# Convolution taps laid out over other steps of a fused convolution and FFN, and put between VectorE's low parts and their sum

## The chip, the cores and the metric

The kernel runs on one core of one Trainium2 chip. Its time is the device time of one execution in microseconds (us). The core has TensorE (matrix products; PE in the profile, its weight loads PEld), VectorE (DVE), ScalarE (ACT), GpSimd (POOL) and SyncE (SP, which here only issues transfers). Each engine takes its instructions in the order in which the program lists them; semaphores hold an instruction until what it needs is there.

## The reference, cut to what matters

```python
def _attn_ref(x, weight):                    # x (8, 4096, 192), weight (8, 7)
    w = weight - np.max(weight, axis=-1, keepdims=True)
    w = np.exp(w)
    w = w / (np.sum(w, axis=-1, keepdims=True) + 1e-09)
    x_pad = np.concatenate([np.zeros((B, pad, D)), x], axis=1)
    idx = np.arange(S)[:, None] + np.arange(K)[None, :]
    x_unf = x_pad[:, idx, :].reshape(B, S, K, H, group)
    out = np.einsum('hk,bskhg->bshg', w, x_unf)

def _moe_ref(x, w_in, w_out):                # (32768, 192), (192, 2048), (2048, 192)
    h = x @ w_in
    g = np.where(h >= 1, h, np.where(h <= -1, 0.0, (h + 1) ** 2 / 4))
    return g @ w_out
```

A causal convolution of seven taps along the sequence, with one set of softmax weights per head, and behind it a two-layer network on every token. All arrays are float32.

## The kernel before, in words

The 32768 tokens are cut into 64 blocks of 512 (`TB`). The 2048 hidden features of a block are taken in eight pairs of 128. One pair of one block is a step `q` of the main loop (512 steps); `j = q % 8` is its place in the block, `c, i = divmod(q, 16)` its place in a pair of blocks. I call the 16 steps of a pair of blocks a period. The convolution for a pair of blocks is done in three units: "a" (the first block's channels 0 to 127), "b" (the second block's) and "r" (the other 64 channels of both).

Float32 precision comes from splitting each operand into a high and a low part of a faster type (`float32r`). The first 16 steps (`NF32`) run the second product in plain float32 while the split weights are made; all later steps have the same shape:

- TensorE, `mm1(q)` (L405): 18 matmuls of 64 rows and 512 columns into a PSUM buffer `h`, of which there are two, so the product of step `q` needs the buffer of step `q-2` to be free again. Then `mm2(q-3)` (L458): 18 matmuls that add the second product of an earlier step into four banks.
- ScalarE, `act_both(q)` (L504): L507 and L508 make `g = ((h+1)/2 clipped at 0) ** 2`. After the last step of a block, `evac_banks` (L547) copies the four banks out (four L552, in steps i = 2 and 10). Then what the convolution asks of it, and `act_hi(q-1)` (L518): the high part `gh`.
- VectorE, `act_lo(q-2)` (L520): L524 takes the low part `gl = g - gh`, L528 adds its two halves to `m`. Then the transposes of the output (L573, in i = 6, 7, 14, 15), what the convolution asks, and last `act_most(q)` (L510, L806), which reads `h` once more and so frees its PSUM buffer.

What the convolution does in a step stands in a plan written by hand: `PLAN_B`, `PLAN_A`, `PLAN_R` (L748 to L751) give for each `i` the taps, "T" (the transpose that brings channels to partitions, L148) or "split". `conv_slot` (L759) carries it out, for b, a and r in this order. Taps of unit a are VectorE's (L213 for the first, L215 for the others). Taps of b and r are a product on ScalarE (L220; L227 for tap 0) and an add on GpSimd (L231). "split" makes the high part on ScalarE (L249, L263) and the low part on GpSimd (L253) or, for r, VectorE (L264), and SP issues the transfers that swap halves between partitions. B's transpose for the coming pair is at the very end of step 15 (L950), and its taps are in steps 0 to 5 of its own pair.

GpSimd's queue also issues the accumulating transfers that join the four banks (`evac_add`, L556, in j = 3 and 4), SP's queue the stores (`store`, L563, in j = 6 and 7) and the loads of x. The first pair of blocks has plans of its own (`FIRST_*`).

The order of the calls within a step of the steady part is what the change touches (L926 to L951):

```python
act_both(q); evac...; act_lo(n); evac_add...; store...
conv_slot(i, conv_b, conv_n.get("a"), conv_n.get("r"))
act_hi(q - 1); act_most(q)
```

Of the kernel before, what the change touches and what calls it, by code (L numbers as in the profile page):

```python
# [8 lines left out]
F32 = mybir.dt.float32  # L9
# [9 lines left out]
P = 128  # L19
TB = 512  # L20
SQ = 32
# [10 lines left out]
def lightconv_then_ffn(ctx: ExitStack, tc: tile.TileContext, x, weight, w_in, w_out, out):  # L32
# [33 lines left out]
    NPAIR = NF // 2  # L66
    DR = D - P
    NG = TB // SQ + 1
# [5 lines left out]
    stage = ctx.enter_context(tc.tile_pool(name="stage", bufs=2))  # L74
# [3 lines left out]
    xw = ctx.enter_context(tc.tile_pool(name="xw", bufs=2))  # L78
# [32 lines left out]
    def load_unit(c, u, engs=None):  # L111
        ta, tb = 2 * c * TB, (2 * c + 1) * TB
        if u == "rb":
            return load_raw([tb, tb, tb + TB // 2, tb + TB // 2], [P, P + SQ, P, P + SQ], engs,
                            TB // 2)
        if u == "r":
            return load_raw([ta, ta, tb, tb], [P, P + SQ, P, P + SQ], engs)
        return load_raw([ta if u == "a" else tb] * 4, [0, SQ, 2 * SQ, 3 * SQ], engs)
# [14 lines left out]
    NF32 = 2 * NPAIR  # L133
    SH = NG * SQ - TB - (K - 1)

    class Conv:
# [5 lines left out]
            self.n = TB // 2 if u == "rb" else TB  # L142

        def transpose(self):
            self.xT = xw.tile([P, NG * SQ], F32, name="xT")
            self.y = xw.tile([P, TB], F32, name="y")
            n = self.n + SQ
            nc.vector.transpose(out=self.xT[:, 0:n],  # L148
                                in_=self.raw.rearrange("p j b -> p (j b)")[:, 0:n])
# [155 lines left out]
    CC = max(n_all)  # L305
# [96 lines left out]
    NQ = NSB * NPAIR  # L402
    hs, g32, gs, ghs, gls, gts, accs = {}, {}, {}, {}, {}, {}, {}

    def mm1(q):  # L405

        s, j = divmod(q, NPAIR)

        if q == 0:
            h = hs[q] = [ps_o.tile([P, TB], F32, name=n) for n in ("accr1", "accm0")]  # L410
        else:
            h = hs[q] = ps_h.tile([P, 2, TB], F32, name="h")
            h = [h[:, e, :] for e in range(2)]

        if s == 0:
            mms = [(WI[j], us, [xop[s][u] for u in us]) for us in ("ns", "sn", "rr")]
        else:
            mms = [(W[j][:, part], u + u, [xop[s][u, x]] * 2) for u in "nsr"
                   for part, x in ((0, "hi"), (1, "hi"), (0, "lo"))]
        for n, (w, us, x) in enumerate(mms):  # L420
            for e in range(2):
                c0 = COL[us[e]][e]
                nc.tensor.matmul(h[e], w[HALVES[e], c0:c0 + P], x[e][e],  # L423
                                 start=(n == 0), stop=(n == len(mms) - 1))
# [5 lines left out]
    def mm2_first(q):  # L430


        s, j = divmod(q, NPAIR)
        g, w = g32.pop(q), WF[j + LAG]
        if j == 0:
            new_accs(s)
        for e in range(2):
            for b in range(TB // P):
                a, c0 = "mr"[b // 2], b % 2 * D
                for i, half in enumerate(HALVES):  # L440
                    nc.tensor.matmul(accs[s][a, i][:, c0:c0 + D], g[half, e, b * P:(b + 1) * P],  # L441
                                     w[half, e, :], start=(j == 0 and e == 0 and b % 2 == 0),
                                     stop=(j == NPAIR - 1 and e == 1 and b % 2 == 1))
# [39 lines left out]
    def tiles(q):  # L483
        return [slice(0, 1), slice(1, 2)] if q == NQ - 1 else [slice(0, 2)]
# [25 lines left out]
    def act_most(q):  # L510
        h, g = hs.pop(q), gs[q]
        for e in tiles(q):
            most(h[:, e, :], g[:, e, :])
# [3 lines left out]
        for e in tiles(q):  # L517
            nc.scalar.copy(gh[:, e, :], gs[q][:, e, :])  # L518

    def act_lo(q):  # L520
        gl = gls[q] = act.tile([P, 2, TB], F32R, name="gl", bufs=3)
        g, gh = gs.pop(q), ghs[q].bitcast(F32)
        for e in tiles(q):
            nc.vector.tensor_sub(gl[:, e, :], g[:, e, :], gh[:, e, :])  # L524
        gt = stage.tile([P, CC], F32R, name="m")[:, 0:TB]
        gts[q] = gt
        gl = gls[q].bitcast(F32)
        nc.vector.tensor_add(gt, gl[:, 0, :], gl[:, 1, :])  # L528
# [188 lines left out]
    def whole(j, *cols):  # L717
        for _ in chunks[j].bits(*cols):
# [20 lines left out]
    conv_b, conv_rb = Conv(0, "b", raw_b), Conv(0, "rb", raw_rb)  # L739
# [5 lines left out]

    PLAN_B = {0: (0, 1), 1: (2,), 2: (3,), 3: (4,), 4: (5, 6), 5: "split"}  # L748
    PLAN_A = {1: ("T",), 2: (0, 1), 3: (2,), 4: (3,), 8: (4,), 9: (5,), 10: (6,), 11: "split"}
    PLAN_R = {5: ("T",), 6: (0,), 7: (1,), 8: (2,), 9: (3,), 10: (4,), 11: (5,), 12: (6,),  # L750
              13: "split"}  # L751


    FIRST_B = {2: 2, 3: 3, 4: 4, 5: 5}
# [1 line left out]
    FIRST_A = {7: ("T", 0, 1, 2), 8: (3, 4), 9: (5, 6), 11: "split"}  # L756
    FIRST_R = {8: ("T",), 9: (0,), 10: (1, 2), 11: (3, 4), 12: (5, 6), 13: "split"}

    def conv_slot(i, b, a, r):  # L759
        early = b.c == 0  # L760
        plans = ((None if early else b, PLAN_B), (a, FIRST_A if early else PLAN_A),
                 (r, FIRST_R if early else PLAN_R))
        for u, plan in plans:
            what = plan.get(i, ()) if u else ()
            if what == "split":
                if u is r:
                    u.split_rest()
                else:
                    u.split()
                continue  # L770
            if "T" in what:
                u.transpose()
            ks = [k for k in what if k != "T"]
            if ks:
                (u.taps_dve if u is a and not early else u.taps)(*ks)
# [8 lines left out]
    def parts_hi(q):  # L784
        for n, rest in PARTS.get(q, ()):
            chunks[n].hi(rest)
# [17 lines left out]
    def most(h, g):  # L804

        nc.vector.scalar_tensor_tensor(out=g, in0=g, scalar=1.0, in1=h, op0=ALU.min, op1=ALU.max)  # L806
# [74 lines left out]
    conv_n, ahead = {}, {}  # L881
    for q in range(NQ + LATE):
        s, j = divmod(q, NPAIR)
        c, i = divmod(q, 2 * NPAIR)
        if q < NQ and i == 0 and c > 0:
            conv_b = conv_n["b"]
        if q < NQ and i == (0 if c > 0 else 4):
            conv_n, ahead = ahead, {}
            if c + 1 < NB:
                for u in "arb":  # L890
                    if u not in conv_n:
                        conv_n[u] = Conv(c + 1, u, load_unit(c + 1, u))
        if i == 14 and c + 2 < NB:
            ahead = {u: Conv(c + 2, u, load_unit(c + 2, u)) for u in "ar"}

        done = q - (DELAY if q < NF32 + DELAY else LATE)
        if done < 0 or q == NF32 + DELAY:
            done = None
        if q == NPAIR:
            mm2_first(done)  # L900
        if q < NQ:
            mm1(q)
        if done is not None and q != NPAIR:
            (mm2 if done >= NF32 else mm2_first)(done)

        if q < 2:
            (step_0, step_1)[q]()
        elif q < NPAIR:
            first_step(q)
        elif q < NF32:  # L910
            if q == NPAIR + 1:
                evac(0)
            if q == 2 * NPAIR - 2:
                pending.extend(late)
            let_go()
            act_clip(q)
            act_square(q)
            parts_hi(q + 1)
            parts_lo(q, (True,))
            let_go()  # L920
            act_max(q)
            parts_lo(q, (False,))
            conv_slot(i, conv_b, conv_n.get("a"), conv_n.get("r"))
            if j >= NPAIR - 2:
                store(0, "mr"[j - NPAIR + 2])
        else:  # L926
            if q < NQ:
                act_both(q)
            if done is not None and done % NPAIR == NPAIR - 1:
                (evac if done < NF32 else evac_banks if done < NQ - 1 else evac_last)(  # L930
                    done // NPAIR)
            if q == NF32:
                parts_lo(q)
            n = q - 1 if q < NF32 + 3 else q - 2
            if n in ghs and n not in gls:
                act_lo(n)
            if q < NQ:
                if s > 2 and j in (3, 4):
                    evac_add(s - 1, j - 3)
                m = 6 if s > 2 else 2  # L940
                if m <= j < m + 2:
                    store(s - 1, "mr"[j - m])
                conv_slot(i, conv_b, conv_n.get("a"), conv_n.get("r"))
            if q - 1 in gs and q - 1 not in ghs:
                act_hi(q - 1)
            if q < NQ:
                act_most(q)
            if q < NF32 + 2:
                act_hi(q)
        if q < NQ and i == 2 * NPAIR - 1 and conv_n:  # L950
            conv_n["b"].transpose()  # L951
        if q == NQ - 4:
            plain = ob.tile([P, TB // SQ, SQ], F32, name="osb").rearrange("p j b -> p (j b)")[:, 0:P]
            diagonal(plain, 0)
# [26 lines left out]
```

## Time and profile before

| | us |
|---|---|
| median of 3 runs | 2159.35 |
| lowest and highest | 2158.59 to 2160.54 |
| the profiled execution | 2159.94 |
| its span, first to last instruction | 2157.9 |
| TensorE busy | 2136.2 |
| VectorE busy | 1996.8 |
| ScalarE busy | 1976.9 |
| GpSimd busy | 824.8 |

The mean granted clock of TensorE is 0.999. Matmuls run in pairs on two halves of the array, so their durations overlap and TensorE's busy time is a union. In a row of the timeline stand the start, the duration, the engine, the line of the kernel, the operation and its operands; a bracket at the end gives the idle time before it and what ended that. Durations on VectorE and ScalarE can overlap by some 0.08 us with the next instruction, so distances from start to start are used for sums. An instruction that waits for more than a semaphore, for a port say, is shown longer.

### The profile page before, as it was taken

The page shows a single profiled execution, that of the slowest core. Times are in us where ns is not written, and L with a number is a line of the kernel's source. Part 1 is how long each engine was busy: PE and PEld are TensorE (multiplying, and loading weights), DVE is VectorE, ACT ScalarE, POOL GpSimd, SP SyncE. Part 2 cuts the span into 40 slices and gives each one's busy share as a digit, 9 for nine tenths or more (in the row PEclk, how much of TensorE's full clock was granted, in tenths as well). Part 3 has the DMA queues.
Part 4 walks back from the last instruction along what each step waited for, and adds up shares of the span by engine and source line. Part 5 has one row for each costly group of instructions (what it writes and reads, how often), then busy time and mean ns, then how long its engine had stood idle before and what let it go on. Part 6 is the DMA issues. An engine that isn't in the chain of part 4 may idle for free.

```text
span 2157.9 us, 46889 instructions
## 1 busy us (share of the span) xinstructions
PE 2136.2 (99%) x18654; PEld 1741.5 (81%) x18654; DVE 1996.8 (93%) x2110; ACT 1976.9 (92%) x2381; POOL 824.8 (38%) x749
## 2 busy tenths in 40 slices
PE   9999999999999999999999999999999999999998
PEld 6988888888788888888888888888888888888887
DVE  8889999999999999999999999999999999999987
ACT  7799999999999999999999999999999999999997
POOL 1534343343343443433434334434244343343341
PEclk9999999999999999999999999999999999999999
DMA  6333343433433333434334333343343343433422
GB/s 166 71 62 56 63 83 68 75 65 56 79 68 73 71 61 67 78 67 78 56 62 84 69 73 67 55 77 69 72 78 58 64 80 68 78 60 56 85 52 45
DMA packets 470155, 151.78 MB, mean 70 GB/s; under 512 B 418800, under 2 KB 426352, under 8 KB 469936
## 3 DMA queue, kind: packets, MB, share of 16 engines
q1 hardware_dynamic: 446352, 108.71, 25.0%
q0 software_dynamic: 23424, 39.99, 12.9%
q8 instruction: 145, 2.38, 0.5%
q14 instruction: 74, 0.61, 0.1%
q10 hardware_dynamic: 160, 0.10, 0.0%
HBM read 32.84 MB, written 25.17 MB: 27 GB/s over the span
## 4 chain that ended last, share of the span: by engine, by line
PE 68%; DVE 24%; issue 6%; ACT 2%; DVEq 0%; POOL 0%; ACTq 0%; POOLq 0%
PE h L423 35%; PE accr L475 20%; PE accm L475 10%; DVE g L806 8%; DVE gl L524 8%; DVE y L215 4%; DVE osb L573 2%; DVE xT L148 1%; PE accm L441 1%; PE accr L441 1%; DVE m L528 1%; ACT gh L518 1%; ACT t L552 0%; ACT p L220 0%; ACT g L507 0%
## 5 line engine op out<-in xcount | busy, mean ns | idle before, releaser
L231 POOL TENSOR_TENSOR y<-y,p 128x512 f32<-128x512 f32 x366 | 513.2, 1402 | 1188.9 <-ACT p L220 1183.0
L524 DVE TENSOR_TENSOR gl<-g,gh 128x1024 fp32r<-128x1024 f32 (+1 forms) x497 | 654.6, 1317 | 78.2 <-ACT gh L518 77.9
L423 PE MATMUL h<-hi,w 64*128 64x512 f32 x4032 | 636.7, 393 | 14.2 <-DVE g L806 14.2
L507 ACT ACTIVATE g<-h 128x1024 f32<-128x1024 f32 (+1 forms) x497 | 508.9, 1024 | 121.8 <-PE h L423 119.0
L806 DVE SCALAR_TENSOR_TENSOR g<-g,h 128x1024 f32<-128x1024 f32 x504 | 606.7, 1204 | 7.7 <-ACT g L508 5.6
L475 PE MATMUL accr<-gh,wg 64*128 64x512 f32 x3968 | 611.6, 386 | 0.0
L508 ACT ACTIVATE g<-g 128x1024 f32<-128x1024 f32 (+1 forms) x497 | 527.2, 1061 | 15.8
L518 ACT CAST gh<-g 128x1024 fp32r<-128x1024 f32 (+1 forms) x497 | 516.5, 1040 | 1.1 <-DVE g L806 1.0
L423 PEld LDWEIGHTS h<-hi,w 64*128 64x128 f32 x4032 | 373.4, 184 | 116.2 <-DVE g L806 43.1
L528 DVE TENSOR_TENSOR m<-gl 128x512 fp32r<-128x512 f32 x496 | 399.0, 805 | 52.9 <-DVE gl L524 1.8
L475 PEld LDWEIGHTS accr<-gh,wg 64*128 64x128 f32 x3968 | 372.0, 184 | 78.1
L423 PE MATMUL h<-lo,w 64*128 64x512 f32 x2016 | 396.9, 387 | 0.0
L475 PE MATMUL accr<-gl,words 64*128 64x512 f32 x1984 | 386.6, 386 | 0.2 <-DVE gl L524 0.2
L475 PE MATMUL accm<-gh,wg 64*128 64x512 f32 x1984 | 305.7, 386 | 0.0
L423 PE MATMUL h<-rh,w 64*128 64x512 f32 x992 | 304.4, 387 | 0.0
L423 PE MATMUL h<-rhi,w 64*128 64x512 f32 x992 | 304.4, 387 | 0.0
L220 ACT ACTIVATE p<-xT,wk 128x512 f32<-128x512 f32 x382 | 270.3, 717 | 0.0
L423 PEld LDWEIGHTS h<-lo,w 64*128 64x128 f32 x2016 | 192.2, 184 | 40.2 <-DMA lo<-lo 0.2
L475 PEld LDWEIGHTS accr<-gl,words 64*128 64x128 f32 x1984 | 186.1, 184 | 39.6 <-DVE gl L524 0.6
L475 PEld LDWEIGHTS accm<-gh,wg 64*128 64x128 f32 x1984 | 186.0, 184 | 38.9
L561 POOL DMA_DIRECT2D t<-t x244 | 206.2, 980 | 22.4 <-ACT t L552 19.3
L423 PEld LDWEIGHTS h<-rhi,w 64*128 64x128 f32 x992 | 182.9, 184 | 19.9
(143 smaller groups left out, 2073.4 us busy)
## 6 DMA issues: line engine op xcount, KB each, us to landing
t<-t POOLq DMA_DIRECT2D x183, 128.0 KB, 3.6
out_dram<-osb SPq DMA_DIRECT2D x366, 64.0 KB, 1.9
raw<-in_x_dram SPq DMA_DIRECT2D x334, 68.0 KB, 2.4
hi<-hi SPq DMA_DIRECT2D x126, 128.0 KB, 2.6
lo<-lo SPq DMA_DIRECT2D x126, 128.0 KB, 2.3
t<-t POOLq DMA_DIRECT2D x61, 256.0 KB, 3.3
rhi<-rh SPq DMA_DIRECT2D x62, 128.0 KB, 2.3
rlo<-rl SPq DMA_DIRECT2D x62, 128.0 KB, 2.2
```

The source lines that it names most:

```text
L215: nc.vector.scalar_tensor_tensor(out=y, in0=tap, scalar=wt, in1=y, op0=ALU.mult, op1=ALU.add)
L220: nc.scalar.mul(p, self.xT[:, SH + k:SH + k + TB], wk[:, self.wsel, k:k + 1])
L231: nc.gpsimd.tensor_add(y, y, self.product(k))
L423: nc.tensor.matmul(h[e], w[HALVES[e], c0:c0 + P], x[e][e], start=(n == 0), stop=(n == len(mms) - 1))
L475: mm = nc.tensor.matmul(accs[s][bank], w[half], g[half], start=(j == 0 and bank not in seen), stop=(j == NPAIR - 1 and k % 3 == 2 and (ban ...
L507: nc.scalar.activation(g[:, e, :], hs[q][:, e, :], AF.Relu, bias=0.5, scale=0.5)
L508: nc.scalar.activation(g[:, e, :], g[:, e, :], AF.Square)
L518: nc.scalar.copy(gh[:, e, :], gs[q][:, e, :])
L524: nc.vector.tensor_sub(gl[:, e, :], g[:, e, :], gh[:, e, :])
L528: nc.vector.tensor_add(gt, gl[:, 0, :], gl[:, 1, :])
L561: nc.gpsimd.dma_start(out=to, in_=src, accum_op=ALU.add)
L806: nc.vector.scalar_tensor_tensor(out=g, in0=g, scalar=1.0, in1=h, op0=ALU.min, op1=ALU.max)
```

## The change

1. `act_lo` is cut in two, `act_low` (L524) and `act_sum` (L528). In a step the call of `conv_slot` now comes between them, so that VectorE's taps, transposes and r's low part lie between low part and sum, and ahead of `evac_add` and `store` in the program. In the steps 18 and 19 `act_most` is called ahead of `conv_slot`.
2. New plans. B's transpose goes to step 12 of the pair before, its taps 0 to 3 to steps 14 and 15 of the pair before, taps 4 to 6 to steps 1 to 3 of its own. A's and r's taps move too. `SECOND_B` keeps the old plan of b for the second pair of blocks.
3. From the third pair on, r takes its transposed input and its sum from two buffers of another pool, so that only a and b rotate through the old ones.

```diff
         def transpose(self):
-            self.xT = xw.tile([P, NG * SQ], F32, name="xT")
-            self.y = xw.tile([P, TB], F32, name="y")
+            if self.u == "r" and self.c > 1:
+                self.xT, self.y = (stage.tile([P, CC], F32, name="r")[:, 0:n]
+                                   for n in (NG * SQ, TB))
+            else:
+                self.xT = xw.tile([P, NG * SQ], F32, name="xT")
+                self.y = xw.tile([P, TB], F32, name="y")
...
-    PLAN_B = {0: (0, 1), 1: (2,), 2: (3,), 3: (4,), 4: (5, 6), 5: "split"}
-    PLAN_A = {1: ("T",), 2: (0, 1), 3: (2,), 4: (3,), 8: (4,), 9: (5,), 10: (6,), 11: "split"}
-    PLAN_R = {5: ("T",), 6: (0,), 7: (1,), 8: (2,), 9: (3,), 10: (4,), 11: (5,), 12: (6,),
-              13: "split"}
+    PLAN_B = {12: ("T",), 14: (0, 1), 15: (2, 3), 1: (4,), 2: (5,), 3: (6,), 5: "split"}
+    PLAN_A = {1: ("T",), 2: (0,), 4: (1,), 7: (2,), 8: (3,), 9: (4,), 10: (5,), 11: (6,),
+              12: "split"}
+    PLAN_R = {2: ("T",), 4: (0,), 6: (1,), 7: (2,), 8: (3, 4), 9: (5,), 11: (6,), 13: "split"}
+    SECOND_B = {0: (0, 1), 1: (2,), 2: (3,), 3: (4,), 4: (5, 6), 5: "split"}
...
-            if n in ghs and n not in gls:
-                act_lo(n)
+            low = n in ghs and n not in gls
+            ahead_of = q in (NF32 + 2, NF32 + 3)
+            if low:
+                act_low(n)
+            if ahead_of:
+                act_most(q)
+            if q < NQ:
+                conv_slot(i, conv_b if i < 8 else conv_n.get("b"), conv_n.get("a"),
+                          conv_n.get("r"))
+            if low:
+                act_sum(n)
             if q < NQ:
                 if s > 2 and j in (3, 4):
                     evac_add(s - 1, j - 3)
                 m = 6 if s > 2 else 2
                 if m <= j < m + 2:
                     store(s - 1, "mr"[j - m])
-                conv_slot(i, conv_b, conv_n.get("a"), conv_n.get("r"))
             if q - 1 in gs and q - 1 not in ghs:
                 act_hi(q - 1)
-            if q < NQ:
+            if q < NQ and not ahead_of:
                 act_most(q)
...
-        if q < NQ and i == 2 * NPAIR - 1 and conv_n:
+        if i == 2 * NPAIR - 1 and c == 0:
             conv_n["b"].transpose()
```

More of the change, by code (lines that the diff above doesn't have):

```diff
@@ L518, in act_hi, with act_low @@
             nc.scalar.copy(gh[:, e, :], gs[q][:, e, :])
-    def act_lo(q):
+    def act_low(q):
         gl = gls[q] = act.tile([P, 2, TB], F32R, name="gl", bufs=3)
@@ L524, in act_lo, with act_sum @@
             nc.vector.tensor_sub(gl[:, e, :], g[:, e, :], gh[:, e, :])
+    def act_sum(q):
         gt = stage.tile([P, CC], F32R, name="m")[:, 0:TB]
@@ L759, in conv_slot @@
     def conv_slot(i, b, a, r):
-        early = b.c == 0
-        plans = ((None if early else b, PLAN_B), (a, FIRST_A if early else PLAN_A),
+        early = b is not None and b.c == 0
+        plans = ((None if early else b, SECOND_B if b and b.c == 1 else PLAN_B),
+                 (a, FIRST_A if early else PLAN_A),
                  (r, FIRST_R if early else PLAN_R))
```

## The prediction

> **What bounds the kernel now.** I read the page, then the list of waits, then sums over stretches, then the timeline of one period (16 steps, two blocks) engine by engine.
>
> ```profile
> PE 2136.2 (99%) x18654; PEld 1741.5 (81%) x18654; DVE 1996.8 (93%) x2110; ACT 1976.9 (92%) x2381; POOL 824.8 (38%) x749
> ```
>
> TensorE is the bound, with VectorE and ScalarE nearly full beside it. So the question is how long TensorE stands still. The first row below holds 28 periods (16128 matmuls are 448 steps of 36), the second nine steps in which TensorE never waits:
>
> ```profile
> 201.31:2058.09 1856.78, 1845.73 (x16128) 1503.05 (x16129) 1737.04 (x1765) 1727.55 (x2045) 729.17 (x637) 1.00 0.39 69
> 1002.17:1038.89 36.72, 36.72 (x326) 30.30 (x326) 33.31 (x36) 33.91 (x40) 14.19 (x17) 1.00 0.51 91
> ```
>
> A free step is 36.72 / 9 = 4.08 us. 448 of them are 1827.8, so the 28 periods lose 1856.8 - 1827.8 = 29.0 us, 1.03 each. The granted clock is 1.00 in both rows: the loss is waiting.
>
> ```profile
> PEld h L423 <- DVE g L806: 43.1, 89, 3.2
> ...
> PE h L423 <- DVE g L806: 14.2, 33, 2.8
> ```
>
> TensorE waits for one thing, VectorE's L806, which frees the PSUM buffer of the first product two steps later. 89 waits are about three a period; the longest, near 3 us, comes once. Where VectorE loses its lead is seen in steps 8 and 9 of a period (each starts at L524; L215 is a tap of A):
>
> ```profile
> 1054.35 1.22 DVE L524 TENSOR_TENSOR gl<-g,gh 128x1024 fp32r<-128x1024 f32 x1
> 1055.68 0.69 DVE L528 TENSOR_TENSOR m<-gl 128x512 fp32r<-128x512 f32 x1
> 1056.28 1.84 DVE L215 SCALAR_TENSOR_TENSOR y<-xT,wk,y 128x512 f32<-128x512 f32 x1
> 1058.05 1.21 DVE L806 SCALAR_TENSOR_TENSOR g<-g,h 128x1024 f32<-128x1024 f32 x1
> 1059.18 1.21 DVE L524 TENSOR_TENSOR gl<-g,gh 128x1024 fp32r<-128x1024 f32 x1
> 1060.49 1.70 DVE L528 TENSOR_TENSOR m<-gl 128x512 fp32r<-128x512 f32 x1
> 1062.12 0.74 DVE L215 SCALAR_TENSOR_TENSOR y<-xT,wk,y 128x512 f32<-128x512 f32 x1
> 1062.78 1.21 DVE L806 SCALAR_TENSOR_TENSOR g<-g,h 128x1024 f32<-128x1024 f32 x1
> ```
>
> ```profile
> 1056.28 1.30 POOL L231 TENSOR_TENSOR y<-y,p 128x512 f32<-128x512 f32 x1 [2.48 <-ACT p L220]
> 1060.35 1.29 POOL L231 TENSOR_TENSOR y<-y,p 128x512 f32<-128x512 f32 x1 [2.78 <-ACT p L220]
> ```
>
> ```profile
> 1064.04 0.74 PE L423 MATMUL h<-hi,w 64*128 64x512 f32 x4 [0.35 <-DVE g L806]
> ```
>
> From L524 to the next L524 step 8 takes 1059.18 - 1054.35 = 4.83, over 4.08 although it holds only four instructions. Each of the two steps has one stretched instruction: L215 1.84 instead of 0.74 (+1.10), L528 1.70 instead of 0.69 (+1.01). Each begins within 0.2 us of one of GpSimd's adds, of two SBUF operands, and ends when that add has. L806 and the transposes, with one SBUF operand, are not stretched. I call this a hold and count up to 1.16 from the add's start. The last L806 ends at 1063.99, and TensorE goes on at 1064.04.
>
> **How much VectorE may lag.** ScalarE in the same step 9:
>
> ```profile
> 1058.54 1.06 ACT L508 ACTIVATE g<-g 128x1024 f32<-128x1024 f32 x1
> 1059.50 0.71 ACT L220 ACTIVATE p<-xT,wk 128x512 f32<-128x512 f32 x1
> 1060.12 1.04 ACT L518 CAST gh<-g 128x1024 fp32r<-128x1024 f32 x1
> 1061.69 1.03 ACT L507 ACTIVATE g<-h 128x1024 f32<-128x1024 f32 x1 [0.54 <-PE h L423]
> ```
>
> I measure a step from 1059.50, where its square (L508) is over. L806 at 1062.78 has lag D = 3.28, and about 0.5 of it was stalled; so D up to about 2.8 is free. Weights load 0.2 to 0.3 ahead of their matmul and wait first: 2.5 is the lower end. From these rows one step leads to the next:
> - ScalarE: L507 1.06, L508 0.96, L518 0.95 (start to start) leave 4.08 - 2.97 = 1.1 a step for products (0.61 each).
> - L524 starts at the later of L518's end (1.07 after its start) and L806's start + 1.13, or when a hold ends.
> - L524 to L528 is 1.31, L528 to the next 0.60, a tap 0.66. GpSimd's add starts 0.85 after its product does (1060.35 - 1059.50) and takes 1.3.
>
> **The change, part by part.** No tap is added or removed. Three things move.
>
> *Between low part and sum.* L528 reads what L524 writes and starts 1.31 after it, while L524 after L806, of the same size, starts 1.13 after it. A tap or transpose in between takes that 0.18 in ten of 16 steps. By the Trainium skill ("VectorE: DVE Perf Modes", section "The DRAIN you can't avoid") no VectorE instruction starts before the pipe of the one before is empty, and order saves nothing. These rows disagree: 1059.18 lies 0.08 before the end of the L806 in front, 1060.49 lies 0.10 behind the end of the L524 in front. I take the row; by the rule, lags would be 0.2 to 0.4 larger around steps 7 to 9.
>
> *The plans.* Durations of what moves or stands in its way:
>
> ```profile
> 1045.02 0.73 DVE L148 STREAM_TRANSPOSE xT<-raw 128x544 f32<-128x544 f32 x1
> ...
> 1048.71 0.70 DVE L573 STREAM_TRANSPOSE osb<-t 128x512 f32<-128x512 f32 x1
> ```
>
> ```profile
> 1063.72 1.07 ACT L552 COPY t<-accr 128x512 f32<-128x512 f32 x2
> 1064.68 1.10 ACT L552 COPY t<-accm 128x512 f32<-128x512 f32 x2
> 1065.63 0.76 ACT L220 ACTIVATE p<-xT,wk 128x512 f32<-128x512 f32 x1
> ```
>
> The evacuation costs ScalarE 1.91 in steps 2 and 10; a tap of R beside it in step 10 goes away. Steps 14, 15 and 0, idle on ScalarE before, take four of B's taps; step 4 is left with one product instead of two. ScalarE then lags most in step 3, by 1.91 + 0.61 - 1.1 = 1.4. On VectorE A's seven taps go from steps 2,2,3,4,8,9,10 to 2,4,7,8,9,10,11, B's transpose from 15 to 12, R's from 5 to 2. Walking the rule through the new plan gives D for steps 0 to 15: 1.4, 0.8, 0.8, 1.8, 1.8, 0.7, 0.8, 1.2, 0.6, 2.8, 2.3, 1.4, 0.9, 1.9, 1.5, 1.3. The critical passage: step 8 has two of R's products; the second add starts at 0.86 + 1.30 + 0.08 = 2.24 after the step's mark and holds to 3.40, so L524 (ready at 2 x 0.61 + 1.07 = 2.29) starts as if at 3.40, which is -0.68 in step 9. Its tap runs from 0.45 to 1.11. Step 9's own add arrives at 0.11 + 0.85 = 0.96 (0.11: ScalarE's lag after two products), inside that tap, and gets the port at its end, as here, where an add that came during L528 went ahead of the tap queued right behind:
>
> ```profile
> 1453.58 0.69 DVE L528 TENSOR_TENSOR m<-gl 128x512 fp32r<-128x512 f32 x1 [0.46 <-DVE gl L524]
> 1454.19 1.79 DVE L215 SCALAR_TENSOR_TENSOR y<-xT,wk,y 128x512 f32<-128x512 f32 x1
> ```
>
> ```profile
> 1453.81 1.62 POOL L231 TENSOR_TENSOR y<-y,p 128x512 f32<-128x512 f32 x1 [2.46 <-ACT p L220]
> ```
>
> L528 then waits to 1.05 + 1.16 = 2.21 and L806 starts at 2.82, against a limit of 2.5 to 2.8: a stall of 0 to 0.3 a period. I take 0.2. All other steps stay 0.2 or more below the limit. So of 1.03 a period 0.83 goes, in 29 periods (28 above and the one before): 24.1 us.
>
> *The step with the long stall*, the second of the second pair, whose L806 now goes ahead of the taps:
>
> ```profile
> 98.79 2.11 DVE L524 TENSOR_TENSOR gl<-g,gh 128x1024 fp32r<-128x1024 f32 x1 [1.58 <-ACT gh L518]
> ...
> 103.81 1.22 DVE L806 SCALAR_TENSOR_TENSOR g<-g,h 128x1024 f32<-128x1024 f32 x1
> ```
>
> ```profile
> 101.77 0.50 PE L475 MATMUL accr<-gl,words 64*128 64x512 f32 x2
> 105.08 1.22 PE L423 MATMUL h<-hi,w 64*128 64x512 f32 x4 [2.80 <-DVE g L806]
> ...
> 108.64 0.62 PE L475 MATMUL accr<-gh,wg 64*128 64x512 f32 x4
> ```
>
> L806 can follow L524 at 100.90 and end at 102.1; the product then starts at about 102.3, 2.8 earlier. It also took 108.64 - 105.08 = 3.56 instead of half a step, 2.04: 1.5 more behind a pause. Together about 4.1 (estimate; 2.8 if the slow product stays, since no row shows it without its pause). The taps there then delay only a sum that TensorE reads a step later.
>
> *What else moves, at no cost.* GpSimd's accumulating transfers and SP's stores now come behind the step's taps in program order. GpSimd is busy 729 of 1857, its transfers end steps ahead of the stores that read them; without that cover each would cost what its add takes, 1.3. In step 13 L264 stands ahead of L528 and waits for L263:
>
> ```profile
> 1010.67 0.60 ACT L263 CAST rh<-y 128x512 fp32r<-128x512 f32 x1
> ```
>
> That, with L264 and L528 behind it, is the lag 1.9 of step 13; L528 and so TensorE's low product wait, below the limit. R's own buffers end the rotation with A and B; no row shows a wait there, so nothing gained or lost.
>
> The sum against the profiled execution (2159.9 us): 2159.9 - 24.1 - 4.1 = 2131.7, given as 2132. The median of the runs shown, 2159.35, lies 0.6 below that execution, which I leave in the range.
>
> **The rivals.** (1) *No stall is left.* The add of step 9 comes 0.15 later than worked out, behind the tap, or VectorE's next instruction keeps the port: L806 of step 9 starts at 1.7. The Trainium skill ("SBUF — State Buffer", section "SBUF: two separate sides") gives the shared pair to whichever starts first for the whole instruction, which leaves a chain of taps without a gap undecided; the rows at 1453 speak against VectorE keeping it. Time: 2159.9 - 29 x 1.03 - 4.1 = 2126. (2) *Order saves nothing* (the rule of the pipe above). VectorE is 0.18 slower in ten steps; step 9 is still set by the hold, but step 10 begins 0.2 later and the stall is 0.4: 2132 + 29 x 0.2 = 2138. The start-to-start rows speak against it. (3) *The stall moves.* Another wait replaces L806, such as the sum behind L264, and costs the same 1.03: only the start gains, 2159.9 - 4.1 = 2155.8. (4) *Slower: two holds in one step.* Tap and sum now stand one behind the other, both with two SBUF operands; if an add comes before each of them in step 9, D is 2.8 + 1.16 = 4.0 and the stall 1.2 to 1.5 a period. It decides from D = 2.5 + 1.03 = 3.5. With 1.4: 2159.9 + 29 x 0.37 - 4.1 = 2166.5. For it: GpSimd has two adds queued in steps 8 and 15. Against it: an add needs a product, 0.61 on ScalarE, and the plan puts one into step 9.
>
> **How the numbers follow.** Forecast 0.56, (1) 0.19, (2) 0.05, (3) 0.08, (4) 0.12. A difference of 0.2%, 4.3 us, is about the least that a measurement of this kernel can tell. Forecast, (1) and (2) are faster: 0.80; (3) is within it: 0.08; (4) slower: 0.12. The range begins at (1)'s 2125, and ends where one further step of lag 1.8 takes a whole hold to 2.96 and stalls 0.45 on top of 0.3: 29 x 0.28 + 4.1 = 12.2 gained, 2148.
>
> **What would show it.** Right: a period near 65.5 us; the list's L806 waits down to at most one a period, in step 9 to 11; no 2.80 wait near 105; L524 to tap 1.13. Stretched instructions remain, since the adds are as many, but now the sum behind a tap is one. Wrong: a period of 66.3 or more, a wait of TensorE on L528's sum, or ScalarE waiting for GpSimd before a split.

## The result, and the profile after

The changed kernel takes 2134.81 us (median of 5 runs, 2134.48 to 2137.08) against 2160.54 us for the kernel before in the same session; the ratio is 0.9885, 95% interval 0.987 to 0.9899. The profiled execution took 2134.48 us, 25.5 less than the one of before. Forecast were 2132 and 27.9 less.

The profile page's row of the engines, the sums over 28 periods (from the product of step 11 of the third pair, as in the row of before), and two rows of the list of waits (total in us, times, longest), all of the changed kernel:

```profile
PE 2124.9 (100%) x18654; PEld 1743.6 (82%) x18654; DVE 1965.4 (92%) x2110; ACT 1979.4 (93%) x2381; POOL 801.8 (38%) x749
```

```profile
195.75:2032.59 1836.84, 1836.84 (x16130) 1506.43 (x16128) 1708.26 (x1765) 1729.99 (x2045) 707.60 (x637) 1.00 0.38 70
```

```profile
PEld h L427 <- DVE g L814: 11.3, 31, 0.4
...
PEld accm L479 <- DVE m L534: 7.0, 31, 0.3
```

A period takes 1836.84 / 28 = 65.60 instead of 66.31, with 65.28 free. (Lines have moved: L806 is now L814, L524 is L528, L528 is L534, L215 is L219, L231 is L235.) TensorE's waits for L814 are 31, one a period, instead of 89, and a new short one, for the sum L534, stands beside each. TensorE's row calls it 100% busy, for a stretched matmul counts as busy; the 0.32 us that a period still loses is seen only in its length.

Where the time went, by the starts of two products: the one at 201.31 before starts at 195.75 now, 5.56 us earlier; the 28 periods behind it are 1856.78 - 1836.84 = 19.94 shorter. Together 25.5, and nothing behind them. But 0.66 of the 5.56 was there at the product of step 8 (38.08 now, 38.74 before), ahead of all that the change touches, and 0.82 at that of step 16, ahead of the long stall. I take this part as spread of the start and not as a gain: in the other kernels of the study, steps 8 to 12 alone take 24.2 to 24.7.

Steps 8 and 9 of a period, now on VectorE, on GpSimd and on ScalarE:

```profile
977.05 2.32 DVE L528 TENSOR_TENSOR gl<-g,gh 128x1024 fp32r<-128x1024 f32 x1 [0.50 <-ACT gh L522]
979.29 0.74 DVE L219 SCALAR_TENSOR_TENSOR y<-xT,wk,y 128x512 f32<-128x512 f32 x1
979.95 1.77 DVE L534 TENSOR_TENSOR m<-gl 128x512 fp32r<-128x512 f32 x1
981.65 1.21 DVE L814 SCALAR_TENSOR_TENSOR g<-g,h 128x1024 f32<-128x1024 f32 x1
982.78 1.21 DVE L528 TENSOR_TENSOR gl<-g,gh 128x1024 fp32r<-128x1024 f32 x1
983.91 0.74 DVE L219 SCALAR_TENSOR_TENSOR y<-xT,wk,y 128x512 f32<-128x512 f32 x1
```

```profile
975.61 2.67 POOL L235 TENSOR_TENSOR r<-r,p 128x512 f32<-128x512 f32 x2 [2.77 <-ACT p L224]
979.79 1.39 POOL L235 TENSOR_TENSOR r<-r,p 128x512 f32<-128x512 f32 x1 [1.50 <-ACT p L224]
```

```profile
978.94 0.71 ACT L224 ACTIVATE p<-r,wk 128x512 f32<-128x512 f32 x1
```

This is the passage that the prediction worked out: step 8's two adds run one behind the other (2.67), the second holds L528 (2.32 instead of 1.21), step 9's add arrives at 979.79 during the tap, goes ahead of the sum queued behind, and holds it (1.77 instead of 0.68). L814 starts 981.65 - 978.94 = 2.71 after the step's mark; 2.82 was worked out. The next product starts at 982.91, right after L814's end. On TensorE:

```profile
977.74 0.39 PE L479 MATMUL accm<-m,words 64*128 64x512 f32 x2
977.97 0.62 PE L479 MATMUL accr<-gh,wg 64*128 64x512 f32 x4
...
981.82 0.46 PE L479 MATMUL accm<-m,words 64*128 64x512 f32 x2
982.12 0.62 PE L479 MATMUL accr<-gh,wg 64*128 64x512 f32 x4
...
982.91 0.73 PE L427 MATMUL h<-hi,w 64*128 64x512 f32 x4
```

From the matmuls that read the sum to the ones behind them it takes 982.12 - 981.82 = 0.30, in the step before 977.97 - 977.74 = 0.23: the wait for the sum costs 0.07 (0.03 to 0.09 in the 28 periods). The rest of the period's 0.32 comes with the wait for L814, about half of it in the first four matmuls behind the wait, which take 0.73 instead of 0.62.

The long stall near 105 us is gone. VectorE and TensorE there:

```profile
97.89 2.11 DVE L528 TENSOR_TENSOR gl<-g,gh 128x1024 fp32r<-128x1024 f32 x1 [1.71 <-ACT gh L522]
99.92 1.21 DVE L814 SCALAR_TENSOR_TENSOR g<-g,h 128x1024 f32<-128x1024 f32 x1
```

```profile
100.95 0.42 PE L479 MATMUL accr<-gl,words 64*128 64x512 f32 x2
101.19 0.74 PE L427 MATMUL h<-hi,w 64*128 64x512 f32 x4
...
103.38 0.64 PE L479 MATMUL accr<-gh,wg 64*128 64x512 f32 x4
```

L814 follows the low part at once, the product starts without a pause and takes 103.38 - 101.19 = 2.19 instead of 3.56. The granted clock over the slow product, from 105.08 to 108.64 in the trace of before, was 0.58; from 101.19 to 103.38 it is 1.00 now.

### The profile page after: what moved, and what is told of

Its sections match the earlier page's. It is cut to its first block, busy times and chain, and to the rows that moved or that the text cites. A ratio compares the mean times of both kernels' runs of the same rounds, so it can differ in the third digit from the quotient of the medians.

```text
span 2132.8 us, 46880 instructions
## 1 busy us (share of the span) xinstructions
PE 2124.9 (100%) x18654; PEld 1743.6 (82%) x18654; DVE 1965.4 (92%) x2110; ACT 1979.4 (93%) x2381; POOL 801.8 (38%) x749
## 4 chain that ended last, share of the span: by engine, by line
PE 99%; ACT 0%; DVE 0%; issue 0%; DVEq 0%; POOL 0%; POOLq 0%; ACTq 0%
PE h L427 49%; PE accr L479 31%; PE accm L479 16%; PE accm L445 1%; PE accr L445 1%; PE accr L195 0%; PE accm L659 0%; PE accr L427 0%; ACT g L512 0%; DVE t L604 0%; DVE gl L528 0%; ACT g L511 0%; PE accm L186 0%; ACT gh L522 0%; PE h L612 0%
## 5 line engine op out<-in xcount | busy, mean ns | idle before, releaser
L528 DVE TENSOR_TENSOR gl<-g,gh 128x1024 fp32r<-128x1024 f32 (+1 forms) x497 | 701.4, 1411 | 75.2 <-ACT gh L522 71.2
L427 PE MATMUL h<-hi,w 64*128 64x512 f32 x4032 | 627.4, 389 | 0.0
L814 DVE SCALAR_TENSOR_TENSOR g<-g,h 128x1024 f32<-128x1024 f32 x504 | 607.4, 1205 | 6.8 <-ACT g L512 4.7
L235 POOL TENSOR_TENSOR y<-y,p 128x512 f32<-128x512 f32 x186 | 243.4, 1309 | 621.7 <-ACT p L224 619.3
L235 POOL TENSOR_TENSOR r<-r,p 128x512 f32<-128x512 f32 x180 | 240.4, 1336 | 513.6 <-ACT p L224 511.3
L534 DVE TENSOR_TENSOR m<-gl 128x512 fp32r<-128x512 f32 x496 | 371.2, 748 | 20.8 <-DVE gl L528 0.5
```

The lines of the kernel that those rows point to most:

```text
L235: nc.gpsimd.tensor_add(y, y, self.product(k))
L427: nc.tensor.matmul(h[e], w[HALVES[e], c0:c0 + P], x[e][e], start=(n == 0), stop=(n == len(mms) - 1))
```

## The experiments

The theory on test, the hold theory: a period loses what L806 lags beyond its limit, and the lag is made by holds, which happen where one of GpSimd's adds meets a VectorE instruction of two SBUF operands that is followed by another. So it is the meeting of plan and order that counts. Rivals: the order gains by itself (A), order saves nothing (B), and others named with each run. All runs have medians beside the kernel before on the same chip.

**The order alone.** The kernel before, with `conv_slot` between `act_low` and `act_sum` in all steps; old plans.

```diff
-                act_lo(n)
+                act_low(n)
+            if q < NQ:
+                conv_slot(i, conv_b, conv_n.get("a"), conv_n.get("r"))
+            if low:
+                act_sum(n)
```

> The kernel before with only the order changed (taps and transposes between low part and sum, in all steps; old plans, no early L806 in steps 18 and 19). Hold theory: the order alone moves the holds but does not remove them, because the old plan still has two products of b in step 4 and r's seventh tap in step 12; walked through, L806 lags 3.5 in step 5 and 2.8 in step 13, so a period still loses about 1 us: 2160 us (2150 to 2166). Rival A, the order is what gains (0.18 us in each step with something in between, more than the 1.03 us a period that TensorE waited): about 2131 us.

Measured: 2179.11 us, ratio 1.0084 (1.0071 to 1.0098), a usual period of 66.9. Neither number came: 2160, the time of the kernel before, was worked out, and it is 18 us slower. Step 5 of a period on VectorE, on GpSimd, and TensorE in step 6:

```profile
914.08 2.31 DVE L524 TENSOR_TENSOR gl<-g,gh 128x1024 fp32r<-128x1024 f32 x1 [0.24 <-ACT gh L518]
916.31 0.73 DVE L148 STREAM_TRANSPOSE xT<-raw 128x544 f32<-128x544 f32 x1
916.97 1.79 DVE L530 TENSOR_TENSOR m<-gl 128x512 fp32r<-128x512 f32 x1
918.68 1.21 DVE L808 SCALAR_TENSOR_TENSOR g<-g,h 128x1024 f32<-128x1024 f32 x1
```

```profile
912.64 2.67 POOL L231 TENSOR_TENSOR y<-y,p 128x512 f32<-128x512 f32 x2 [0.23 <-ACT p L220]
...
916.65 1.55 POOL L253 TENSOR_TENSOR lo<-y,hi 128x512 fp32r<-128x512 f32 x1
```

```profile
918.81 0.50 PE L475 MATMUL accm<-m,words 64*128 64x512 f32 x2 [0.75 <-DVE m L530]
```

The stall comes from step 5, as in the walk: the low part is held by the double add, the sum by b's split. But L808 lags only 918.68 - 915.96 = 2.72 there (at 915.96 ScalarE is done with the step's square), not 3.5. What the walk missed is who waits: TensorE stops for the sum, in the middle of its second product, and then once more for L808; its step 6 takes 5.22 instead of 4.08. Rival A is out: with the old plans the order costs 18 us.

**The plans without the order.** The changed kernel with `conv_slot` behind sum and store.

```diff
-            if q < NQ:
-                conv_slot(i, conv_b if i < 8 else conv_n.get("b"), ...)
             if low:
                 act_sum(n)
...
                     store(s - 1, "mr"[j - m])
+                conv_slot(i, conv_b if i < 8 else conv_n.get("b"), ...)
```

> The changed kernel with the taps and transposes back behind the sum (new plans, early L806 in steps 18 and 19). Hold theory: the plans carry the gain; in step 9 the add now falls into the sum and holds the tap, L806 lags 3.0 instead of 2.8, stall 0.2 a period more: 2140 us (2135 to 2145). Rival A, the order is what gains: nearly all of the steady gain is lost, about 2155 us. Rival B, order saves nothing (no VectorE instruction starts before the pipe is empty): 2135 us as with the change.

Measured: 2139.51 us, ratio 0.9902 (0.9889 to 0.9916). The number is the hold theory's; rival A's 2155 is out, and rival B's 2135 lies below all four runs (2139.03 to 2140.55). The plans carry most of the gain, the order 4.7 us. (The early L806 is in this kernel too, and so are r's own buffers, whose part no run shows by itself.)

But the stall is not 0.2 more in every period, as worked out. Step 8's low part and second add are shown starting within 0.03 us of each other, and either can go first. Two neighbouring periods on VectorE and GpSimd:

```profile
715.50 1.22 DVE L528 TENSOR_TENSOR gl<-g,gh 128x1024 fp32r<-128x1024 f32 x1
716.83 1.60 DVE L534 TENSOR_TENSOR m<-gl 128x512 fp32r<-128x512 f32 x1
...
781.06 2.36 DVE L528 TENSOR_TENSOR gl<-g,gh 128x1024 fp32r<-128x1024 f32 x1
783.53 0.69 DVE L534 TENSOR_TENSOR m<-gl 128x512 fp32r<-128x512 f32 x1
```

```profile
714.05 3.82 POOL L235 TENSOR_TENSOR r<-r,p 128x512 f32<-128x512 f32 x2 [2.36 <-ACT p L224]
779.61 2.73 POOL L235 TENSOR_TENSOR r<-r,p 128x512 f32<-128x512 f32 x2 [2.37 <-ACT p L224]
```

(Each row of GpSimd holds both adds of step 8.) In the first period the low part goes ahead, the second add waits and then holds the sum; 13 of 28 periods are like this and take 65.6, as with the change. In the second period the add goes ahead and holds the low part; 14 periods are like this and take 65.8. One takes 67.52. So the 4.7 us of the order are 0.2 in half of the periods, and some 1.9 of one odd period.

**The early L806 alone**, in steps 18 and 19 of the kernel before (`if ahead_of: act_most(q)` behind the low part).

> The kernel before with only L806 of steps 18 and 19 ahead of the taps. The long wait near 105 us and the slow product behind it go, nothing else: 4.4 us, 2156 us, and the periods stay at 66.3 us. Rival: the pause is taken elsewhere in the first periods, and the time stays at 2160 us.

Measured: 2157.67 us, ratio 0.9987 (0.9977 to 0.9996), 3.1 us less; 4.4 were worked out. In its trace the product of step 21 starts 4.1 us earlier than in that of before, that of step 32 only 2.6: a part is given back at once with the old plans. Usual periods are 66.3 as before.

**r's taps spread.** The changed kernel with

```diff
-    PLAN_R = {2: ("T",), 4: (0,), 6: (1,), 7: (2,), 8: (3, 4), 9: (5,), 11: (6,), 13: "split"}
+    PLAN_R = {2: ("T",), 4: (0, 1), 6: (2,), 7: (3,), 8: (4,), 9: (5,), 11: (6,), 13: "split"}
```

> The changed kernel with r's taps spread so that no step from 6 on has two of its products: 4: 0 and 1, 6: 2, 7: 3, 8: 4, 9: 5, 11: 6. Hold theory: L806 of step 9 lags 0.5 instead of 2.7, the largest lag is 1.9, and the stall that the change leaves (0.32 us a period, 65.60 instead of 65.28) goes: 2134.8 - 30 x 0.32 = 2125 us. Rival C, what is left comes from another wait (ScalarE's evacuation in step 10, or the sum that TensorE reads): 2135 us, period 65.6.

Measured: 2127.97 us, ratio 0.9848 (0.9834 to 0.9861): the fastest kernel of the study that does all the work. 26 of 29 periods take 65.28 us, the free length. Steps 8 and 9 on VectorE, and GpSimd:

```profile
971.37 0.75 DVE L219 SCALAR_TENSOR_TENSOR y<-xT,wk,y 128x512 f32<-128x512 f32 x1
972.03 0.69 DVE L534 TENSOR_TENSOR m<-gl 128x512 fp32r<-128x512 f32 x1
972.64 1.21 DVE L814 SCALAR_TENSOR_TENSOR g<-g,h 128x1024 f32<-128x1024 f32 x1
973.77 1.22 DVE L528 TENSOR_TENSOR gl<-g,gh 128x1024 fp32r<-128x1024 f32 x1
974.90 0.75 DVE L219 SCALAR_TENSOR_TENSOR y<-xT,wk,y 128x512 f32<-128x512 f32 x1
975.57 0.68 DVE L534 TENSOR_TENSOR m<-gl 128x512 fp32r<-128x512 f32 x1
976.17 1.22 DVE L814 SCALAR_TENSOR_TENSOR g<-g,h 128x1024 f32<-128x1024 f32 x1
```

```profile
972.39 1.48 POOL L235 TENSOR_TENSOR r<-r,p 128x512 f32<-128x512 f32 x1 [2.77 <-ACT p L224]
976.48 1.30 POOL L235 TENSOR_TENSOR r<-r,p 128x512 f32<-128x512 f32 x1 [2.60 <-ACT p L224]
```

The adds now fall into the sum or into L814; what stands behind is L814, which is not held, and no VectorE instruction of these two steps is stretched; the low part of step 10 is, by 0.33, by the end of the second add. GpSimd waits instead, 0.18 us in the first row. Rival C is out.

**Without the add of step 9.** The changed kernel, r's tap 5 not added.

> The changed kernel without GpSimd's add of r's tap 5 (step 9); its product on ScalarE stays, so the output lacks that tap for r from the third pair on. Hold theory: the add of step 9 is what holds the sum there; without it L806 of step 9 lags about 1.4 instead of 2.5 and the stall of 0.32 us a period goes, period 65.28: 2125 us. Rival C, ScalarE's load around the evacuation or the sum's new place makes the stall: period 65.6, 2135 us.

Measured: 2127.42 us, ratio 0.9851 (0.9838 to 0.9865); 28 of 29 periods 65.28. One add of 1.3 us on an engine that is busy 38% makes the whole remaining stall.

**r's split behind the sum** in step 13 (`act_sum` ahead of `split_rest`, taps as in the changed kernel).

> The changed kernel with r's split in step 13 behind the sum, so that VectorE no longer waits for ScalarE's L267 with the sum queued behind (31 waits of 1.4 us in the trace of the changed kernel). Hold theory: the lag of step 13, 1.6, is under the limit, so taking that wait away gains nothing: 2135 us, period 65.6. Rival D, a wait of an engine that is busy 92% costs what it takes: 29 x 1.4 = 40 us at most, a third of it at least.

Measured: 2135.48 us, ratio 0.9888 (0.9875 to 0.9902), periods of 65.6. In its list of waits L268's wait is 20.7 us in total instead of 44.1, so it is halved, not gone, and the 23 us taken away have gained nothing. Rival D is out.

**r's taps spread, taps behind the sum.** The order of before in the fastest plan.

> r's taps spread as in the run that did so, and the taps and transposes behind the sum as before the change. Hold theory: with no step that has two adds running into the next one, no lag comes near the limit in either order, so the order is worth nothing: 2128 us, period 65.28 to 65.35. Rival A, the order itself is worth its 0.18 us in ten steps: a loss of the size seen between the two orders of the changed plans, 4.7 us, or more: 2133 us.

Measured: 2184.40 us, ratio 1.0115 (1.0102 to 1.0129), usual periods 66.6 or 67.6. Both numbers worked out were wrong: with this plan the order is worth 56 us. Step 7 and part of step 8 on VectorE and GpSimd:

```profile
990.80 0.71 DVE L579 STREAM_TRANSPOSE osb<-t 64x512 f32<-64x512 f32 x1
991.54 1.54 DVE L219 SCALAR_TENSOR_TENSOR y<-xT,wk,y 128x512 f32<-128x512 f32 x1
993.01 1.21 DVE L814 SCALAR_TENSOR_TENSOR g<-g,h 128x1024 f32<-128x1024 f32 x1
994.14 1.21 DVE L528 TENSOR_TENSOR gl<-g,gh 128x1024 fp32r<-128x1024 f32 x1
995.46 1.70 DVE L534 TENSOR_TENSOR m<-gl 128x512 fp32r<-128x512 f32 x1
```

```profile
991.23 1.31 POOL L235 TENSOR_TENSOR r<-r,p 128x512 f32<-128x512 f32 x1 [2.34 <-ACT p L224]
995.32 1.30 POOL L235 TENSOR_TENSOR r<-r,p 128x512 f32<-128x512 f32 x1 [2.78 <-ACT p L224]
```

The add starts during the transpose, 0.31 ahead of the tap, and holds it. The lag so made puts the next add on the end of the low part, where it holds the sum, and so on. To see whether one add starts this, the next run leaves it out.

**The same without the add of step 7** (r's tap 3).

> The run with spread taps behind the sum, without GpSimd's add of r's tap 3 in step 7 (its product stays; the output lacks that tap for r from the third pair on). Hold theory: that add is the seed; it holds the tap of step 7 by 0.8 us, the lag of 2.3 then puts each next add on the low part, and each of the steps 8 to 12 gets a hold of its own. Without this one add of 1.3 us all of them go: period 65.3 instead of 67.6, 2128 us. Rival E, each add costs its own hold wherever it is: one hold less, period 66.8, about 2160 us.

Measured: 2172.36 us, ratio 1.0056 (1.0039 to 1.0073), usual periods 66.9. The theory's number was wrong; rival E's period came out, though not its time. The trace shows why: the row of holds begins one step later, which saves only its first stall. Step 8:

```profile
990.84 1.86 DVE L219 SCALAR_TENSOR_TENSOR y<-xT,wk,y 128x512 f32<-128x512 f32 x1
```

```profile
990.85 1.30 POOL L237 TENSOR_TENSOR r<-r,p 128x512 f32<-128x512 f32 x1 [6.42 <-ACT p L224]
```

The tap is shown 0.01 us ahead of the add and yet held by 1.1: the next add took the part of the one left out.

**The order alone, without b's tap 6** in step 4 (the second of the double add).

> The run with the order alone (old plans), without GpSimd's add of b's tap 6 in step 4 (its product stays; the output lacks that tap for b from the third pair on). Hold theory: the second add of step 4 holds the low part of step 5, and b's split there holds the sum; without it the 1.26 us wait of step 6 goes and the 0.28 us of step 14 stays: period 65.6, 2141 us. Rival F, TensorE waits in step 6 because the sum stands behind the transpose: the period stays at 66.9 us, 2179 us.

Measured: 2141.14 us, ratio 0.9911 (0.9896 to 0.9926), usual periods 65.6. Both holds of step 5 and the wait of step 6 are gone with that one add: 38 us. Rival F is out.

**Spread, behind the sum, without the adds of steps 7, 8 and 9.**

> The run with spread taps behind the sum, without GpSimd's adds of r's taps 3, 4 and 5 (steps 7, 8 and 9; their products stay; the output lacks those taps for r from the third pair on). Where the add of step 7 alone was left out, the add of step 8 came within 0.01 us of the tap's start and held it, with the same lags one step later. If any add that meets a tap standing directly ahead of L806 starts the row of holds, then without the three no lag passes 1.6 and the period is 65.28: 2128 us. Rival E, each add costs its own hold wherever it is: three holds fewer than 67.6, about 65.3 too in steps 7 to 9, but the stalls of steps 11 to 13 (0.4 to 0.5 each) stay: 66.3, 2155 us.

Measured: 2125.89 us, ratio 0.9839 (0.9824 to 0.9854), all 29 periods 65.28, where rival E had 66.3. The stalls of steps 11 to 13 go with them, though the add of step 11 stays: they were the lag handed on.

**Spread, behind the sum, ahead of the output's transposes.**

> The run with spread taps behind the sum, with the taps ahead of the output's transposes instead of behind them. Hold theory: in step 7 the add then meets the tap in progress and the transpose behind it, no hold; but in steps 8 and 9, which have no such transpose, the tap still stands directly ahead of L806 and the add of step 8 holds it as in the run without the add of step 7: period 66.9, 2172 us. Rival G, it was the place of the tap behind the transposes alone that cost: period 65.28, 2128 us.

Measured: 2172.44 us, ratio 1.0056 (1.0039 to 1.0072). Steps 7 and 8, the tap of each and what it meets:

```profile
986.95 0.75 DVE L219 SCALAR_TENSOR_TENSOR y<-xT,wk,y 128x512 f32<-128x512 f32 x1
...
991.54 1.85 DVE L219 SCALAR_TENSOR_TENSOR y<-xT,wk,y 128x512 f32<-128x512 f32 x1
```

```profile
987.47 1.38 POOL L235 TENSOR_TENSOR r<-r,p 128x512 f32<-128x512 f32 x1 [2.32 <-ACT p L224]
991.55 1.29 POOL L235 TENSOR_TENSOR r<-r,p 128x512 f32<-128x512 f32 x1 [2.70 <-ACT p L224]
```

In step 7 the add falls into the tap and a transpose stands behind: no hold. In step 8 it meets the tap's start and holds it. Time and place as worked out; rival G is out.

## Why the prediction was right, step by step

*The bound and the place of the stall: right.* The walk gave one step of sixteen beyond the limit, step 9, with a lag of 2.82; the trace has 2.71 there, and the run without that step's add shows that it makes the whole stall. (Its sum has a slip: it lets the tap end at 1.11 but counts the hold from 1.05; from 1.11 the lag would be 2.88.)

*The size of the stall left: mis-sized.* "I take 0.2" a period; it is 65.60 - 65.28 = 0.32, and the second pair has it too. The 28 periods gained 19.94 instead of 28 x 0.83 = 23.2. The prediction's range for this term, 0 to 0.3, ended just short of it. The main reason is the limit, taken as 2.5 to 2.8 because "about 0.5" of the lag of 3.28 was stalled before. In that trace the products of steps 10 and 11 of the period take 4.73 and 4.26 instead of 4.08: 0.65 to 0.83 was stalled, so the limit was 2.45 to 2.6, and 2.71 - 0.32 = 2.4 fits its lower end. The other part is the wait for the sum: held itself, it comes late for the second product of the step, as the run of the order alone shows in the large. The prediction had named such a wait as a sign of being wrong; it came in every period, but costs only 0.07.

*The long stall: right, with luck at the start.* Up to 195.75 the kernel gained 5.56; worked out were 4.1 and one period's 0.83. What I take for spread of the start is 0.82 of it, the steps from 16 to 27 with the long stall 4.23, and the period behind them 0.51. (The two parts named for the stall, 2.8 and 1.5, make 4.3 and not 4.1.) The early L806 by itself measured 3.1. Without the 0.82 the gain is 24.6 where 27.9 were forecast.

*Between low part and sum.* The tap starts 1.13 behind L528 now (982.78 to 983.91), where the sum started 1.31 behind it. So order does save 0.18 where the next instruction does not read the result of the one in front, and rival (2) is out. The rule of the Trainium skill ("VectorE: DVE Perf Modes", section "The DRAIN you can't avoid") that the next instruction does not start until the pipe is empty does not stand against these rows, as the prediction had it: the same paragraph adds that "A next op that is not held starts earlier", which fits them. But the 0.18 was not what the order is worth. The prediction booked it as a saving of VectorE time; the runs show that order decides which instruction an add meets: +18 us with the old plans, -4.7 with the new ones, -56 with the spread ones.

*No cost of the wait in step 13: right*, by the run with the split behind the sum.

*The rivals.* (1) did not come true: VectorE's queued instruction does not keep the port; in step 9 the add that comes during the tap goes ahead of the sum (979.95) in all 29 periods from the third pair on. The Trainium skill ("SBUF — State Buffer", section "SBUF: two separate sides") gives the shared pair to whichever starts first for its whole instruction and leaves open who is first between two queued VectorE instructions; in this case it was the waiting add. (3) did not come true either: the periods gained, and what TensorE waits for the sum is small. (4), a further hold on top of the two that the prediction had worked out for step 9 (low part and sum), did not come in the changed kernel: in three of the 29 periods tap and sum of step 9 are both held, but then the low part in front of them is not, and L814 starts no later. Rows of such holds, 1.1 us each, are what made four of the other kernels slower than before.

## What to carry to other kernels

Where two engines share a port, the sum of their work does not tell the time; walk the schedule and ask for each instruction of the less busy engine which instruction of the other it meets and what is queued behind that. A lag that sends the next add onto the next two-operand instruction keeps itself going, so one add of 1.3 us per period, on an engine that is busy 38%, cost 7 to 38 us in all here, and moving three taps by a step or two gained 6.8. An order is not good or bad by itself: test it with the plan it is to run with.

## What was not expected of the hardware

An add shown 0.01 us later than the tap that it meets still goes first, and the tap is stretched from 0.74 to 1.86. In that trace (the run without the add of step 7) 37 taps start within 0.06 us of an add. In 36 the add goes first, shown up to 0.034 later than the tap; in one, at 1539.73, it is shown 0.040 later, the tap takes 0.74 and the add 1.86, and the period 66.08 instead of 66.9. So starts in the trace do not tell exactly who has the port, and a schedule that depends on such a meeting depends on hundredths of a microsecond. Single periods of some kernels are 0.7 to 1.9 us longer for once; one of them, in the run with r's taps spread, shows the output's transpose waiting for an accumulating transfer that the prediction had ending steps ahead:

```profile
1194.41 0.72 DVE L579 STREAM_TRANSPOSE osb<-t 128x512 f32<-128x512 f32 x1 [1.63 <-DMA t<-t]
```
